# Threshold attention and a projection pair on one core: every other early slot's weights transposed by TensorE, copies to VectorE, loads and casts moved

## The chip, the core and the metric

The kernel runs on one core of a Trainium2 chip. A core has TensorE (PE: matrix products, results into PSUM), VectorE (DVE), ScalarE (ACT), GpSimd (POOL) and SyncE (SP), each with its own in-order queue, and 16 DMA engines that serve every queue. PSUM is divided into banks, which this kernel gives out by hand. The metric is the device time of one execution in microseconds (us); the median over several runs counts.

## What is computed

Eight batches of eight heads, 576 positions, head size 64. Attention keeps only the keys whose score is within tau of the row's maximum; the heads are put side by side and go through two projections with a hard swish between them.

```python
scores = scale * np.matmul(q, k.transpose(0, 1, 3, 2))
thresh = np.max(scores, axis=-1, keepdims=True) - tau
scores = np.where(scores >= thresh, scores, -1000000000.0)
scores = scores - np.max(scores, axis=-1, keepdims=True)
attn = np.exp(scores)
attn = attn / (np.sum(attn, axis=-1, keepdims=True) + 1e-09)
attn_out = np.matmul(attn, v)
# x: [8 * 576, 8 * 64], heads side by side
h = x @ w_in                      # [4608, 2048]
relu6 = np.clip(h + 3.0, 0.0, 6.0)
out = (h * relu6 / 6.0) @ w_out   # [4608, 512], float32
```

## The kernel before

Four heads of one batch form a *quad* (16 of them), two heads a *pair*. A quad has nine *slots*: slots 0 to 3 are the four tiles of 128 query rows of its first pair, 4 to 7 those of its second, and slot 8 holds the last 64 rows of both pairs. The main loop (L394) walks over all 144 slots, n from 0 to 143, and writes down by hand the order in which each engine gets its work; the tile framework only adds the semaphores. All engines run in order, so what is written earlier in the loop stands ahead on its engine.

In slot n the loop issues: the exponentials of slot n-1 (`sm_exp`, L262, ScalarE); the copy of slot n's scores out of PSUM with their row maximum (`sm_max`, L249, VectorE) and from it the bias of the mask (L252, GpSimd); if a batch is ready, one item of the first projection (`mm1` L315, `mm1_relu` L324/L326, `mm1_gate` L332); the reciprocal of slot n-1's sums (`sm_recip`, L265, VectorE); parts of the second projection (`mm2_part` L344, `mm2_out` L352); the mask of slot n (`sm_mask`, L257, ScalarE); one of the transposes of the next queries or keys, or a product of weights and values; the scores of slot n+1 (`scores`, L228/L234, TensorE); the scaling of slot n-1's weights to bf16 (`sm_norm`, L270, GpSimd) and their transpose.

That last transpose turns `pn`, 128 query rows by 2 x 576 keys in bf16, into nine blocks with keys on the partitions. It is one `dma_start_transpose` on SP's queue for each slot (L277), into `pts[pair]` or, for slot 8, `ptr[quad]`. Attention's second product reads these: `av_main(pair)` in slot 8 for a quad's first pair and in slot 3 of the next quad for its second pair, `av_rest(quad)` in slot 4 of the next quad (`av`, L285/L288).

Queries and keys of the first two batches are transposed by TensorE against an f32 identity (`main_pe` L185, `transpose_rest` L203/L205). `transpose_q` evicts with VectorE (L192), `transpose_k` and the keys of `transpose_rest` with ScalarE (L198, L210, L211). In slots 1, 2 and 5 to 7 of a quad this prepares the pairs to come.

PSUM: `ps_s` has two tiles of two banks for scores, `ps_h` one tile of two banks for the first projection, `ps_o` one bank for the second projection, `ps_m` one bank that transposes of queries and keys and the products with values share. The first projection has its first item in slot 23 (quad 2, slot 5), when the first batch is through; the second projection starts in slot 31. Until then `ps_h` and, but for one transpose ahead of the loop, `ps_o` stand unused.

Loads are queued as jobs and started at the end of a slot: `loads` on SP (two jobs a slot for n < 3, then one), `vcasts` (values, cast to bf16 on the way) and `casts` (16 pieces of w_in, then 16 of w_out) on GpSimd. GpSimd issues such a DMA in its own order, so the next slot's biases stand behind it. `load_quad(1)` queues its jobs in slot 0, `load_quad(quad + 2)` in slot 4 of each quad, `load_v(b + 1)` in slot 0 of each batch's second quad. Outputs wait in `late` and go out on SP in `flush`.

Of the kernel before, what the change touches and what calls it, by code (L numbers as in the profile page):

```python
# [9 lines left out]
F32 = mybir.dt.float32  # L10
BF16 = mybir.dt.bfloat16
# [4 lines left out]
P = 128  # L16
# [5 lines left out]
def kernel(  # L22
# [10 lines left out]
    nc = tc.nc  # L33
    B, H, S, D = q.shape
# [5 lines left out]
    NQUAD = B * H // 4  # L40
    NSLOT = 9
    NB = 2
    scale = 1.0 / math.sqrt(D)
    tau = float(tau)

    singles = ctx.enter_context(tc.tile_pool(name="singles", bufs=1))
# [4 lines left out]
    pn_pool = ctx.enter_context(tc.tile_pool(name="pn", bufs=4))  # L51
# [7 lines left out]
    ps_s = ctx.enter_context(tc.psum_pool(name="ps_s", bufs=2))  # L59
    ps_h = ctx.enter_context(tc.psum_pool(name="ps_h", bufs=1))  # L60
    ps_o = ctx.enter_context(tc.psum_pool(name="ps_o", bufs=1))
    ps_m = ctx.enter_context(tc.psum_pool(name="ps_m", bufs=1))
# [3 lines left out]
    nat = {}  # L66
    vsb = {}
    qkT = {}
    pts = {}
    ptr = {}  # L70
    xT = {}
    loads = []
    casts = []
    vcasts = []
# [3 lines left out]
    def load_quad(quad):  # L78
# [14 lines left out]
        def load_q(n):  # L93
            if b < NB:
                for a in range(2):
# [51 lines left out]
    def start(jobs, n):  # L147
        for _ in range(min(n, len(jobs))):
            jobs.pop(0)()
# [5 lines left out]

    identf = singles.tile([P, P], F32)
    make_identity(nc, identf)
    three = singles.tile([P, 1], F32)
    nc.vector.memset(three[:], 3.0)

# [6 lines left out]
    def alloc_qk(quad):  # L167
        qkT[quad] = (qk_pool.tile([P, 2, S], F32, tag="qT", name="qT"),
                     qk_pool.tile([P, 2, S + 64], F32, tag="kT", name="kT"))
# [4 lines left out]
    def kT_of(pair):  # L174
        return qkT[pair // 2][1][:, pair % 2, :]


    def by_pe(pair):
        return pair // NPAIR < NB

    def main_pe(src, pair, pool):
        ps = pool.tile([P, 512], F32, tag="m" if pool is ps_m else "o", name="tp")
        n = pair % 2
        for t in range(4):
            nc.tensor.transpose(ps[:, t * P:(t + 1) * P], src[:, t, 2 * n:2 * n + 2, :], identf[:])  # L185
        return ps

    def transpose_q(pair, pool=ps_m):
        nq = nat[pair // 2][0]
        if by_pe(pair):  # L190
            ps = main_pe(nq[:, 0:1024].rearrange("p (t h d) -> p t h d", h=4, t=4), pair, pool)
            return lambda: nc.vector.tensor_copy(out=qT_of(pair)[:, 0:512], in_=ps[:])  # L192
        n = pair % 2
        nc.vector.transpose(out=qT_of(pair), in_=nq[:, n * S:(n + 1) * S])

    def transpose_k(pair):
        ps = main_pe(nat[pair // 2][1], pair, ps_m)
        return lambda: nc.scalar.copy(out=kT_of(pair)[:, 64:576], in_=ps[:])  # L198

    def transpose_rest(quad):  # L200
        ps = ps_m.tile([P, 512], F32, tag="m", name="tr")
        nq, _, kr = nat[quad]
        nc.tensor.transpose(ps[:, 0:P], kr[:], identf[:])  # L203
        if by_pe(2 * quad):
            nc.tensor.transpose(ps[:, P:2 * P], nq[:, 1024:1152], identf[:])  # L205

        def evict():
            qT, kT = qkT[quad]
            both = ps[:].rearrange("p (w n t) -> p w n t", n=2, t=64)
            nc.scalar.copy(out=kT[0:64, :, S:S + 64], in_=both[0:64, 0])  # L210
            nc.scalar.copy(out=kT[64:P, :, 0:64], in_=both[64:P, 0])  # L211
            if by_pe(2 * quad):
                nc.vector.tensor_copy(out=qT[:, :, 512:S], in_=both[:, 1])  # L213
        return evict
# [49 lines left out]
    def sm_recip(sl):  # L264
        nc.vector.reciprocal(out=sl.rinv[:], in_=sl.rsum[:])  # L265

    def sm_norm(sl):
        pn = pn_pool.tile([P, 2, S], BF16, tag="pn", name="pn")
        for i in range(2):
            nc.gpsimd.tensor_scalar(out=pn[:, i, :], in0=sl.s[:, i, :], scalar1=sl.rinv[:, i:i + 1], scalar2=1.0,  # L270
                                    op0=Alu.mult, op1=Alu.mult)
        if sl.slot < 8:
            pair, t = 2 * sl.quad + sl.slot // 4, sl.slot % 4
            dst = pts[pair][:, :, t * P:(t + 1) * P]
        else:
            dst = ptr[sl.quad][:, :, :]
        nc.sync.dma_start_transpose(out=dst, in_=pn[:].rearrange("p a b -> p (a b)"))  # L277


    def av(ps, pair, pT, cols):  # L280
# [9 lines left out]
    def av_main(pair):  # L290
        b, hp = divmod(pair, NPAIR)
        if hp == 0:
            xT[b] = x_pool.tile([P, KI, S], BF16, tag="xT", name="xT")
        ps = ps_m.tile([P, 512], F32, tag="m", name="av")
        av(ps[:], pair, pts[pair], slice(0, 512))
        o0 = 64 if b % 2 else 0
        nc.vector.tensor_copy(out=xT[b][:, hp, o0:o0 + 512], in_=ps[:])  # L297

    def av_rest(quad):
        b, g = divmod(quad, 2)  # L300
        ps = ps_m.tile([P, 512], F32, tag="m", name="ar")
        for n in range(2):
            av(ps[:, n * 64:(n + 1) * 64], 2 * quad + n, ptr[quad], slice(n * 64, (n + 1) * 64))
        o0 = 0 if b % 2 else 512
        nc.vector.tensor_copy(out=xT[b][:, 2 * g:2 * g + 2, o0:o0 + 64],
                              in_=ps[:, 0:P].rearrange("p (a b) -> p a b", a=2))
# [69 lines left out]
        return items  # L376

    alloc_qk(0)
    evict = transpose_k(0)
    evict_q = transpose_q(0, ps_o)  # L380
    evict()
    evict_q()
    transpose_rest(0)()

    queue = []
    for quad in range(NQUAD):
        for slot in range(NSLOT):
            sl = Slot()
            sl.quad, sl.slot = quad, slot
            queue.append(sl)  # L390
    queue[0].tiles = scores(0, 0)

    prev = None
    for n, sl in enumerate(queue):  # L394
        quad, slot = sl.quad, sl.slot
        b, g = divmod(quad, 2)
        if slot in (0, 4):
            pts[2 * quad + slot // 4] = pt_pool.tile([P, 9, 512], BF16, tag="pT", name="pT")
        if slot == 8:
            ptr[quad] = ptr_pool.tile([P, 9, P], BF16, tag="pR", name="pR")  # L400
        if quad == 0 and slot == 0:
            load_quad(1)
        if slot == 4 and quad + 2 < NQUAD:
            load_quad(quad + 2)
        if slot == 0 and g == 1 and b + 1 < B:
            load_v(b + 1)
        if prev is not None:
            for i in range(2):
                sm_exp(prev, i)
        sm_max(sl)  # L410

        if slot != 8 and todo1:
            item, then = todo1.pop(0)
            h = mm1(item)
            r = mm1_relu(h, on_act=(slot in (0, 1, 3, 5)))
            mm1_gate(item, h, r)
            todo2.extend(then)
        if prev is not None:
            sm_recip(prev)
        outs = []  # L420
        for _ in range((2, 1, 1, 0, 1, 1, 1, 1, 1)[slot]):
            if todo2:
                bb, mt, part = todo2.pop(0)
                mm2_part(bb, mt, part)
                if part == 3:
                    outs += mm2_out(bb, mt, on_act=False)
        for i in range(2):
            sm_mask(sl, i)
        evict = None
        nxt = 2 * quad + 2  # L430
        if slot == 1:
            evict = transpose_q(2 * quad + 1)
        elif slot == 2:
            evict = transpose_k(2 * quad + 1)
        elif slot == 3 and quad > 0:
            av_main(2 * quad - 1)
        elif slot == 4 and quad > 0:
            av_rest(quad - 1)
            if quad % 2 == 0:
                todo1.extend(moe_of(quad // 2 - 1))  # L440
        elif slot in (5, 6, 7) and quad + 1 < NQUAD:
            if slot == 5:
                alloc_qk(quad + 1)
                evict = transpose_q(nxt)
            elif slot == 6:
                evict = transpose_k(nxt)
            else:
                evict = transpose_rest(quad + 1)
        elif slot == 8:
            av_main(2 * quad)  # L450
        if evict:
            evict()
        if n + 1 < len(queue):
            queue[n + 1].tiles = scores(queue[n + 1].quad, queue[n + 1].slot)
        if prev is not None:
            sm_norm(prev)
        flush()
        late.extend(outs)
        start(loads, 2 if n < 3 else 1)
        start(vcasts, 1 if n else 0)  # L460
        if n > 6:
            start(casts, 1 if n < 22 else 2)
        prev = sl

    for i in range(2):
# [6 lines left out]
    count = [0, 0]  # L472
# [59 lines left out]
```

## Time and profile before

| | us |
|---|---|
| median of 11 runs | 572.95 |
| lowest and highest | 571.73, 575.76 |
| the profiled execution, its time | 575.53 |
| the profiled execution, its span | 573.8 |
| PE busy in the span | 532.7 (93%) |
| ACT busy | 473.1 (82%) |
| DVE busy | 414.1 (72%) |
| POOL busy | 305.6 (53%) |

The span runs from the first to the last instruction of the program. Shares are averages over stages with different limits: the first slots, in which there is no projection yet, and those after the first batch. The slices of the page show it (each digit is a fortieth of the span, 14.3 us, in tenths; PEclk is the granted TensorE clock, DMA the share of the 16 DMA engines):

```profile
PE   6976788889999999998999999998999999999997
...
ACT  3987889688898999997898999988898999984440
...
PEclk9787889899999999999999999999999999999999
DMA  5999999998479787988489877988599775554101
```

The granted clock is below full in the first eight slices and the DMA engines are all but always busy there; from then on TensorE is at nine tenths.

| row of the page | count | busy, us | mean, ns |
|---|---|---|---|
| L228 PE, scores | 1024 | 181.0 | 451 |
| L249 DVE, scores out and maximum | 288 | 206.0 | 752 |
| L257 ACT, mask | 288 | 207.0 | 766 |
| L262 ACT, exponential | 288 | 192.9 | 672 |
| L270 POOL, scaling to bf16 | 288 | 211.6 | 745 |
| L185 PE, f32 transposes of keys | 128 | 20.9 | 289 |

The transposes by DMA are listed with the issues: 128 of pT, 3.5 us in the median from issue to landing.

### The profile page before, as it was taken

What the parts mean: (1) busy time and instruction counts of PE and PEld (TensorE: products, weight loads), DVE (VectorE), ACT (ScalarE), POOL (GpSimd) and SP (SyncE); (2) the same over time, 40 slices, a digit from 0 to 9 for tenths busy, and PEclk for the clock granted to TensorE, in tenths of its full rate; (3) what the DMA queues carried; (4) which work ended last, traced back from release to release, by engine and by line L of the source; (5) the groups of instructions that cost most, each with busy time, mean ns of one, the idle gap of its engine ahead of it and who ended that gap; (6) DMA issues with size and microseconds to landing.
All of it is one profiled execution on the core that took longest, in us unless ns stands there. A gap on an engine that the chain in (4) does not pass through costs nothing.

```text
span 573.8 us, 11332 instructions
## 1 busy us (share of the span) xinstructions
PE 532.7 (93%) x3700; PEld 303.9 (53%) x3700; DVE 414.1 (72%) x1020; ACT 473.1 (82%) x1008; POOL 305.6 (53%) x646
## 2 busy tenths in 40 slices
PE   6976788889999999998999999998999999999997
PEld 3543444554555555554555555554555555655663
DVE  2564557667887879886888888796878888884440
ACT  3987889688898999997898999988898999984440
POOL 0867778765556645654556655654556556552000
PEclk9787889899999999999999999999999999999999
DMA  5999999998479787988489877988599775554101
GB/s 119 142 163 169 186 180 164 183 187 168 98 141 183 130 141 154 165 156 159 90 162 156 156 140 156 187 134 146 108 172 152 152 150 97 128 88 111 39 19 74
DMA packets 298043, 80.45 MB, mean 140 GB/s; under 512 B 281088, under 2 KB 293376, under 8 KB 297984
## 3 DMA queue, kind: packets, MB, share of 16 engines
q1 hardware_dynamic: 280576, 70.81, 66.5%
q0 software_dynamic: 17408, 8.92, 12.8%
q8 instruction: 29, 0.48, 0.3%
q14 instruction: 30, 0.25, 0.1%
HBM read 36.70 MB, written 9.44 MB: 80 GB/s over the span
## 4 chain that ended last, share of the span: by engine, by line
PE 52%; ACT 12%; DVE 11%; issue 4%; DMA 3%; POOL 2%; SPq 1%; DVEq 0%; POOLq 0%
PE h L315 16%; PE o L344 15%; PE s L228 14%; DVE s L249 5%; ACT s L257 4%; ACT s L262 4%; PE av L285 3%; DVE g L332 2%; ACT r L324 2%; DVE r L326 2%; DMA pR<-pn 2%; DMA nq<-in_q_dram 2%; PE tp L185 1%; POOL pn L270 1%; DVE osb L352 1%
## 5 line engine op out<-in xcount | busy, mean ns | idle before, releaser
L270 POOL TENSOR_SCALAR pn<-s,rinv 128x576 bf16<-128x576 f32 x288 | 211.6, 745 | 135.3 <-DVE rinv L265 61.9
L249 DVE TENSOR_SCALAR_CACHE_REDUCE s<-s 128x576 f32<-128x576 f32 x288 | 206.0, 752 | 54.4 <-PE s L228 44.0
L257 ACT ACTIVATE s<-s,bias 128x576 f32<-128x576 f32 x288 | 207.0, 766 | 39.8 <-POOL bias L252 38.7
L262 ACT ACTIVATE s<-s 128x576 f32<-128x576 f32 x288 | 192.9, 672 | 0.4
L228 PE MATMUL s<-kT,qT 64*128 64x288 f32 x1024 | 181.0, 451 | 4.2 <-DVE s L249 3.4
L315 PE MATMUL h<-xT,w_in_sb 128*128 128x320 bf16 (+1 forms) x1024 | 145.8, 288 | 6.1 <-DVE g L332 5.2
L344 PE MATMUL o<-w_out_sb,g 128*128 128x512 bf16 x576 | 141.2, 379 | 6.5 <-DVE osb L352 5.9
L228 PEld LDWEIGHTS s<-kT,qT 64*128 64x128 f32 x1024 | 100.4, 196 | 64.6 <-DVE s L249 26.9
L315 PEld LDWEIGHTS <-w_in_sb 128*128 128x128 bf16 x1024 | 92.3, 98 | 69.8 <-issue 32.0
L332 DVE SCALAR_TENSOR_TENSOR g<-r,h 128x512 bf16<-128x512 f32 (+1 forms) x128 | 96.4, 755 | 41.4 <-ACT r L324 39.6
L252 POOL TENSOR_SCALAR bias<-m 128x1 f32<-128x1 f32 x288 | 54.7, 190 | 78.8 <-DVE s L249 57.4
L344 PEld LDWEIGHTS <-g 128*128 128x128 bf16 x576 | 55.5, 98 | 61.4 <-issue 13.2
L324 ACT ACTIVATE r<-h,three 128x640 f32<-128x640 f32 (+1 forms) x74 | 54.4, 736 | 27.1 <-PE h L315 26.5
L262 ACT ACTIVATION_READ_ACCUMULATOR s<-s 128x1 f32 x288 | 54.3, 189 | 0.0
L285 PE MATMUL av<-pT,vm 128*64 128x512 bf16 x256 | 36.0, 405 | 11.4 <-DVE qT L213 5.2
L326 DVE TENSOR_SCALAR r<-h 128x512 f32<-128x512 f32 (+1 forms) x54 | 40.5, 750 | 0.0
L285 PEld LDWEIGHTS <-vm 128*64 128x64 bf16 x512 | 18.9, 112 | 38.1 <-issue 26.6
L352 DVE TENSOR_SCALAR osb<-o 128x512 f32<-128x512 f32 x31 | 21.0, 676 | 22.2 <-PE o L344 22.2
L265 DVE RECIPROCAL rinv<-rsum 128x2 f32<-128x2 f32 x144 | 22.9, 159 | 12.2 <-ACT s L262 11.4
L297 DVE CAST xT<-av 128x512 bf16<-128x512 f32 x32 | 21.8, 682 | 9.3 <-PE av L288 9.2
L185 PE MATMUL tp<-identf,km 128*128 128x128 f32 x128 | 20.9, 289 | 4.8 <-DMA km<-in_k_dram 4.8
L249 DVE DVE_READ_ACCUMULATOR s<-s 128x1 f32 x288 | 23.9, 83 | 0.0
(34 smaller groups left out, 202.3 us busy)
## 6 DMA issues: line engine op xcount, KB each, us to landing
km<-in_k_dram SPq DMA_DIRECT2D x64, 128.0 KB, 3.0
out_dram<-osb SPq DMA_DIRECT2D x32, 256.0 KB, 2.4
nq<-in_q_dram SPq DMA_DIRECT2D x96, 72.0 KB, 2.7
vm<-in_v_dram POOLq DMA_DIRECT2D x16, 256.0 KB, 5.1
nq<-in_q_dram SPq DMA_DIRECT2D x16, 128.0 KB, 3.4
pT<-pn SPq DMA_TRANSPOSE x128, 3.5
w_in_sb<-in_moe_w_in_dram POOLq DMA_DIRECT2D x16, 128.0 KB, 4.5
w_out_sb<-in_moe_w_out_dram POOLq DMA_DIRECT2D x16, 128.0 KB, 5.1
```

The source lines that it names most:

```text
L228: nc.tensor.matmul(tiles[a][:, hf, 0:HALF], qT_of(pair)[a * 64:(a + 1) * 64, t * P:(t + 1) * P], keys(pair, a, hf), start=True, stop=True)
L249: nc.vector.tensor_scalar(out=sl.s[:, i, :].rearrange("p (a b) -> p a b", a=2), in0=ps[:, :, 0:HALF], scalar1=1.0, scalar2=None, op0=Alu.m ...
L252: nc.gpsimd.tensor_scalar(out=sl.bias[:, i:i + 1], in0=sl.m[:, i:i + 1], scalar1=-scale, scalar2=tau, op0=Alu.mult, op1=Alu.add)
L257: nc.scalar.activation(out=s, in_=s, func=Act.Prelu, bias=sl.bias[:, i:i + 1], scale=scale, alpha=REJECT)
L262: nc.scalar.activation(out=s, in_=s, func=Act.Exp, accum_out=sl.rsum[:, i:i + 1])
L270: nc.gpsimd.tensor_scalar(out=pn[:, i, :], in0=sl.s[:, i, :], scalar1=sl.rinv[:, i:i + 1], scalar2=1.0, op0=Alu.mult, op1=Alu.mult)
L285: nc.tensor.matmul(ps[a * 64:(a + 1) * 64, :], vm[:, 2 * hp + a, c * D:(c + 1) * D], pT[:, 5 * a + c, cols], start=(c == 0), stop=False)
L315: nc.tensor.matmul(hps[:, n, 0:w], w_in_sb[:, ki, (ni + n) * P:(ni + n + 1) * P], xT[b][:, ki, c0:c0 + w], start=(ki == 0), stop=(ki == KI ...
L324: nc.scalar.activation(out=r, in_=hps, func=Act.Relu, bias=three[:])
L326: nc.vector.tensor_scalar(out=r, in0=hps, scalar1=3.0, scalar2=0.0, op0=Alu.add, op1=Alu.max)
L332: nc.vector.scalar_tensor_tensor(out=gbuf[:, ni:ni + 2, c0:c0 + w], in0=r, scalar=6.0, in1=hps, op0=Alu.min, op1=Alu.mult)
L344: nc.tensor.matmul(o_ps[0], gbuf[:, ni, mt * P:(mt + 1) * P], w_out_sb[:, ni, :], start=(ni == 0), stop=(ni == NI - 1))
```

## The change

The weights of every odd slot among the first 22 (n = 1, 3, ... 21) are no longer transposed by DMA. `pe_transpose`, called two slots later between the projection's item and the reciprocal, has TensorE transpose the nine blocks of `pn` against a bf16 identity into the two banks of `ps_h`, and VectorE copies all 1152 columns out in one instruction behind the reciprocal. The other slots keep their DMA transpose.

`bank` replaces the fixed `ps_m`: while n < 28 the transposes of queries and keys and the products with values take `ps_o` and `ps_m` in turn. `copy_out` moves the evictions of the keys from ScalarE to VectorE for 0 <= n < 22.

Ahead of the loop TensorE gets 14 f32 transposes of the identity with a result that nothing reads, and four more between the first keys and the first queries. GpSimd copies one column of the first transposed keys into `gate`, and behind it starts all four loads of the first batch's values. In the loop values are then started only for n > 12; pieces of w_in and w_out are started from n = 0, two a slot for n < 4 and one from there (before: none up to n = 6, one up to n = 21, then two). `load_quad(2)` is called in slot 8 of quad 0 instead of slot 4.

```diff
--- before.py
+++ after.py
@@ -40,6 +40,8 @@
     NQUAD = B * H // 4
     NSLOT = 9
     NB = 2
+    N1 = 22
+    N2 = 28
     scale = 1.0 / math.sqrt(D)
     tau = float(tau)
 
@@ -155,6 +157,16 @@
 
     identf = singles.tile([P, P], F32)
     make_identity(nc, identf)
+
+    warm = ps_s.tile([P, 2, 512], F32, tag="s", name="warm")
+
+    def warm_up(count):
+        for _ in range(count):
+            nc.tensor.transpose(warm[:, 0, 0:P], identf[:], identf[:])
+
+    warm_up(14)
+    identb = singles.tile([P, P], BF16)
+    nc.vector.tensor_copy(out=identb[:], in_=identf[:])
     three = singles.tile([P, 1], F32)
     nc.vector.memset(three[:], 3.0)
 
@@ -174,31 +186,48 @@
     def kT_of(pair):
         return qkT[pair // 2][1][:, pair % 2, :]
 
+    now = -1
+    turn = 0
+
+    def bank(name):
+        nonlocal turn
+        turn += 1
+        if now < N2 and turn % 2:
+            return ps_o.tile([P, 512], F32, tag="o", name=name)
+        return ps_m.tile([P, 512], F32, tag="m", name=name)
+
+
+    def copy_out(out, in_):
+        if 0 <= now < N1:
+            nc.vector.tensor_copy(out=out, in_=in_)
+        else:
+            nc.scalar.copy(out=out, in_=in_)
+
 
     def by_pe(pair):
         return pair // NPAIR < NB
 
-    def main_pe(src, pair, pool):
-        ps = pool.tile([P, 512], F32, tag="m" if pool is ps_m else "o", name="tp")
+    def main_pe(src, pair):
+        ps = bank("tp")
         n = pair % 2
         for t in range(4):
             nc.tensor.transpose(ps[:, t * P:(t + 1) * P], src[:, t, 2 * n:2 * n + 2, :], identf[:])
         return ps
 
-    def transpose_q(pair, pool=ps_m):
+    def transpose_q(pair):
         nq = nat[pair // 2][0]
         if by_pe(pair):
-            ps = main_pe(nq[:, 0:1024].rearrange("p (t h d) -> p t h d", h=4, t=4), pair, pool)
+            ps = main_pe(nq[:, 0:1024].rearrange("p (t h d) -> p t h d", h=4, t=4), pair)
             return lambda: nc.vector.tensor_copy(out=qT_of(pair)[:, 0:512], in_=ps[:])
         n = pair % 2
         nc.vector.transpose(out=qT_of(pair), in_=nq[:, n * S:(n + 1) * S])
 
     def transpose_k(pair):
-        ps = main_pe(nat[pair // 2][1], pair, ps_m)
-        return lambda: nc.scalar.copy(out=kT_of(pair)[:, 64:576], in_=ps[:])
+        ps = main_pe(nat[pair // 2][1], pair)
+        return lambda: copy_out(kT_of(pair)[:, 64:576], ps[:])
 
     def transpose_rest(quad):
-        ps = ps_m.tile([P, 512], F32, tag="m", name="tr")
+        ps = bank("tr")
         nq, _, kr = nat[quad]
         nc.tensor.transpose(ps[:, 0:P], kr[:], identf[:])
         if by_pe(2 * quad):
@@ -207,8 +236,8 @@
         def evict():
             qT, kT = qkT[quad]
             both = ps[:].rearrange("p (w n t) -> p w n t", n=2, t=64)
-            nc.scalar.copy(out=kT[0:64, :, S:S + 64], in_=both[0:64, 0])
-            nc.scalar.copy(out=kT[64:P, :, 0:64], in_=both[64:P, 0])
+            copy_out(kT[0:64, :, S:S + 64], both[0:64, 0])
+            copy_out(kT[64:P, :, 0:64], both[64:P, 0])
             if by_pe(2 * quad):
                 nc.vector.tensor_copy(out=qT[:, :, 512:S], in_=both[:, 1])
         return evict
@@ -265,16 +294,26 @@
         nc.vector.reciprocal(out=sl.rinv[:], in_=sl.rsum[:])
 
     def sm_norm(sl):
-        pn = pn_pool.tile([P, 2, S], BF16, tag="pn", name="pn")
+        sl.pn = pn = pn_pool.tile([P, 2, S], BF16, tag="pn", name="pn")
         for i in range(2):
             nc.gpsimd.tensor_scalar(out=pn[:, i, :], in0=sl.s[:, i, :], scalar1=sl.rinv[:, i:i + 1], scalar2=1.0,
                                     op0=Alu.mult, op1=Alu.mult)
         if sl.slot < 8:
             pair, t = 2 * sl.quad + sl.slot // 4, sl.slot % 4
-            dst = pts[pair][:, :, t * P:(t + 1) * P]
+            sl.dst = pts[pair][:, :, t * P:(t + 1) * P]
         else:
-            dst = ptr[sl.quad][:, :, :]
-        nc.sync.dma_start_transpose(out=dst, in_=pn[:].rearrange("p a b -> p (a b)"))
+            sl.dst = ptr[sl.quad][:, :, :]
+        if not sl.on_chip:
+            nc.sync.dma_start_transpose(out=sl.dst, in_=pn[:].rearrange("p a b -> p (a b)"))
+
+
+    def pe_transpose(sl):
+        ps = ps_h.tile([P, 2, 1024], BF16, tag="h", name="pt")
+        ps = ps[:].rearrange("p a b -> p (a b)")[:, 0:2 * S].rearrange("p (c t) -> p c t", t=P)
+        pn = sl.pn[:].rearrange("p a b -> p (a b)")
+        for c in range(9):
+            nc.tensor.transpose(ps[:, c, :], pn[:, c * P:(c + 1) * P], identb[:])
+        return lambda: nc.vector.tensor_copy(out=sl.dst, in_=ps)
 
 
     def av(ps, pair, pT, cols):
@@ -291,14 +330,14 @@
         b, hp = divmod(pair, NPAIR)
         if hp == 0:
             xT[b] = x_pool.tile([P, KI, S], BF16, tag="xT", name="xT")
-        ps = ps_m.tile([P, 512], F32, tag="m", name="av")
+        ps = bank("av")
         av(ps[:], pair, pts[pair], slice(0, 512))
         o0 = 64 if b % 2 else 0
         nc.vector.tensor_copy(out=xT[b][:, hp, o0:o0 + 512], in_=ps[:])
 
     def av_rest(quad):
         b, g = divmod(quad, 2)
-        ps = ps_m.tile([P, 512], F32, tag="m", name="ar")
+        ps = bank("ar")
         for n in range(2):
             av(ps[:, n * 64:(n + 1) * 64], 2 * quad + n, ptr[quad], slice(n * 64, (n + 1) * 64))
         o0 = 0 if b % 2 else 512
@@ -376,17 +415,23 @@
         return items
 
     alloc_qk(0)
+    gate = singles.tile([P, 1], F32)
     evict = transpose_k(0)
-    evict_q = transpose_q(0, ps_o)
+    warm_up(4)
+    evict_q = transpose_q(0)
     evict()
     evict_q()
     transpose_rest(0)()
+
+    nc.gpsimd.tensor_copy(out=gate[:], in_=kT_of(0)[:, 64:65])
+    start(vcasts, 4)
 
     queue = []
     for quad in range(NQUAD):
         for slot in range(NSLOT):
             sl = Slot()
             sl.quad, sl.slot = quad, slot
+            sl.on_chip = len(queue) < N1 and len(queue) % 2 == 1
             queue.append(sl)
     queue[0].tiles = scores(0, 0)
 
@@ -394,13 +439,14 @@
     for n, sl in enumerate(queue):
         quad, slot = sl.quad, sl.slot
         b, g = divmod(quad, 2)
+        now = n
         if slot in (0, 4):
             pts[2 * quad + slot // 4] = pt_pool.tile([P, 9, 512], BF16, tag="pT", name="pT")
         if slot == 8:
             ptr[quad] = ptr_pool.tile([P, 9, P], BF16, tag="pR", name="pR")
         if quad == 0 and slot == 0:
             load_quad(1)
-        if slot == 4 and quad + 2 < NQUAD:
+        if slot == (4 if quad else 8) and quad + 2 < NQUAD:
             load_quad(quad + 2)
         if slot == 0 and g == 1 and b + 1 < B:
             load_v(b + 1)
@@ -415,8 +461,11 @@
             r = mm1_relu(h, on_act=(slot in (0, 1, 3, 5)))
             mm1_gate(item, h, r)
             todo2.extend(then)
+        copies = pe_transpose(queue[n - 2]) if n > 1 and queue[n - 2].on_chip else None
         if prev is not None:
             sm_recip(prev)
+        if copies:
+            copies()
         outs = []
         for _ in range((2, 1, 1, 0, 1, 1, 1, 1, 1)[slot]):
             if todo2:
@@ -457,9 +506,8 @@
         flush()
         late.extend(outs)
         start(loads, 2 if n < 3 else 1)
-        start(vcasts, 1 if n else 0)
-        if n > 6:
-            start(casts, 1 if n < 22 else 2)
+        start(vcasts, 1 if n > 12 else 0)
+        start(casts, 2 if n < 4 else 1)
         prev = sl
 
     for i in range(2):
```

## The prediction

> **What bounds the kernel now.** I read the stages first: a single-number share of the span mixes two regimes. Columns: length, busy us of PE, PE's weight loads, VectorE (DVE), ScalarE (ACT) and GpSimd (POOL) with instruction counts, granted TensorE clock, DMA share, GB/s.
>
> ```profile
> 10.00:38.00 28.00, 24.52 (x112) 13.62 (x109) 16.14 (x48) 25.24 (x55) 18.20 (x39) 0.88 0.92 153
> 38.00:71.00 33.00, 24.74 (x138) 13.96 (x138) 17.13 (x51) 25.97 (x59) 23.74 (x50) 0.79 1.20 170
> 71.00:84.00 13.00, 10.53 (x51) 5.71 (x50) 7.54 (x22) 12.76 (x29) 10.70 (x22) 0.88 1.06 169
> 84.00:103.00 19.00, 15.77 (x117) 9.06 (x114) 12.42 (x34) 15.32 (x34) 14.53 (x30) 0.86 1.29 176
> 137.00:514.00 377.00, 368.63 (x2715) 209.94 (x2713) 311.99 (x762) 340.58 (x735) 209.89 (x446) 1.00 0.78 143
> ```
>
> From 137 to 514 us TensorE is busy 368.63 of 377 us at full clock: it is the bound, and the change doesn't touch it (3.49 us a slot, 108 slots). By VectorE's maxima (L249) slots 0 to 21 run from 10.4 to 84.6 us, 74.2 us, 3.37 a slot: here no engine is full, the clock is granted at 0.79 to 0.88, and the DMA share exceeds 1. The projections start at slot 23, so the time of slots 0 to 21 lies wholly before the bound stage and comes off the end one for one.
>
> Next, who waits in 10 to 85 us (total, times, longest):
>
> ```profile
> DVE s L249 <- PE s L228: 13.3, 13, 1.9
> ACT s L257 <- POOL bias L252: 11.1, 11, 2.8
> PE av L285 <- DMA pT<-pn: 4.1, 2, 2.4
> PE av L285 <- DVE qT L213: 3.2, 2, 1.8
> PEld L285 <- DMA pR<-pn: 2.5, 1, 2.5
> ```
>
> ScalarE is the busiest (63.97 of the 74 us from 10 to 84), its idle time ends on bias, bias on VectorE's maximum, that on the scores. What makes the scores late shows in the timeline (start, length, engine, instruction):
>
> ```profile
> 45.14 4.96 SPq L277 DMA_TRANSPOSE pR<-pn  x1
> ...
> 50.20 9.21 SPq L277 DMA_TRANSPOSE pT<-pn  x4
> ...
> 50.29 1.92 PE L285 MATMUL av<-pT,vm 128*64 128x512 bf16 x8 [2.42 <-DMA pT<-pn]
> ...
> 55.44 1.45 ACT L257 ACTIVATE s<-s,bias 128x576 f32<-128x576 f32 x2 [2.80 <-POOL bias L252]
> ```
>
> TensorE's queue is in order: attention's second product waits for a transposed tile that the DMA rings deliver late (5.3 us median to landing up to 137 us, 11.2 at worst, against 3.4 afterwards), and the next scores stand behind it. Slots 12, 13 and 21 stretch to 6.7, 4.7 and 6.2 us that way.
>
> **The change, part by part.** Sums are against the profiled execution: span 573.8 us, 575.53 with what lies around it, 2.6 above the median of 572.95; a difference carries over to the median.
>
> *Half the transposes leave DMA.* Eleven of the first 22 (odd slots). Each is 128x1152 bf16, 1152 rows of 256 B; at the DMA queues' mean of 23 ns a packet that is 26 us of packet time, 1.65 us of all 16 engines, so 18 us of a ring that is over-full here. It also takes eleven blocking SP issues away, ahead of which loads and the other transposes queue. I expect the landings to fall to about 4 us and the waits at slots 12, 13 and 21 to go. On ScalarE these were 2.8, 1.9 and 1.7 us: **-4.7 in slots 0 to 21, -1.7 in slot 22.** What is late next: ScalarE itself.
>
> *TensorE gets 11 x 9 bf16 transposes.* No row shows one. Nearest are four f32 ones (L185): 0.44 us on the chain of waits at full clock, 1.11 at half; and a 128-column bf16 weight load, 98 ns (L344). Nine cost 0.9 us at full clock, 1.9 at half. The Trainium skill, "TensorE: Matmul & The Clock Gate", Part 4, speaks against this: about 275 ns for one 128x128 bf16 transpose in a kernel. By that 11 x 9 x 0.275 = 27 us, more than all that there is to win; but L185's mean of 289 ns is such a duration too, and four take 0.44 us from first to last, because they are pipelined. I take 0.9 (bounds 0.9 and 2.5), 10 us over 11 slots. Does it fit? TensorE's work per quad at full clock: nine slots of scores at 1.24 (timeline, from 88.7 us) = 11.2; four f32 transposes at 0.6 and two small ones, 2.9; two main products at 1.45 and a rest one, 3.5; 4.5 transposed slots, 4.0. That is 21.6, 2.4 a slot: inside ScalarE's cycle, if the clock is full.
>
> *VectorE copies them out, 11 x 1152 bf16 from PSUM,* and takes over key copies. From PSUM, 128x512 f32 took 0.69 us and 128x128 0.29 (L192, L213): 1.04 ns an element and 0.16 fixed, so 1.36 us for 1152. "VectorE: DVE Perf Modes", "Why PSUM operands drop a tier", allows two a cycle with 16-bit elements from PSUM: 0.76. No row here shows a 16-bit PSUM source; I take 0.76, because both ends of the copy are bf16 with unit runs, and keep 1.36. VectorE per quad: maxima 9 x 1.45, reciprocals 1.45, query copies 1.65, key copies 1.86, products out 1.67, new copies 4.5 x 0.76 = 3.4: 23.1, or 2.6 a slot; at 1.36 it is 2.9, just over ScalarE's 2.73. Queued behind the copy, which waits for TensorE, are the query and key evictions and the next maximum. The loop exponential, reciprocal, GpSimd's scaling (1.5), transposes (0.9), scores, maximum, bias, mask sums to about 9 us for three slots, 3.0 a slot in the slots concerned. I book **+2.0** for such waits over 22 slots (bounds 0 and 6).
>
> *ScalarE's key copies go* for slots 0 to 21: five of 0.58 and four of 0.25 us, 3.9 us of the engine with the least slack (63.97 - 3.9 = 60.1, 2.73 a slot): **-3.9**.
>
> *Alternating banks* in slots 0 to 27. Today the product of slot 8 waits in ps_m for the small evictions that stand behind ScalarE's masks: "PE av L285 <- DVE qT L213" in slots 8, 17 and 26, 5.2 us in all. The first two are partly counted above; slot 26 gives **-1.5**.
>
> *Casts smoothed.* A w_in issue takes GpSimd 0.57 us. Four first v issues (0.83, 0.83, 0.65, 0.65) move ahead of slot 0, behind the gate on kT, near 7 us; they end near 10, ahead of the first bias at 11.24: hidden with 1 us to spare, and 1 us late at most if that cover goes. Slots 0 to 3 then carry two casts, 1.15 instead of 0.65 to 0.93: with two biases (0.38) and scaling (1.47) 3.0 us a slot against 2.3 to 3.3 now, **+0.8**. In slots 22 to 30 one cast instead of two saves GpSimd 0.57 a slot, where bias makes ScalarE wait 7.2 us (84 to 137 us) and products and projections share the cold stretch from 97.9 to 104.7 us: **-2.5**. The third quad's loads start four slots later, at slot 8, and are due at slot 14: hidden.
>
> *Warm-up.* Fourteen f32 transposes before the data, four between keys and queries. At 0.278 us each they run from about 1.4 to 5.3 us, and the keys landed at 4.77: half a us late, then 1.1 us for the four, +1.5 if the clock stays low. If they raise it, the first scores take 1.5 instead of 2.97 us and slots 0 and 1 gain: -3. The same page says that transpose mode doesn't count as busy for the clock. Around the clock's changes this trace has:
>
> ```profile
> 19.40:22.80 3.40, 2.30 (x11) 1.26 (x10) 2.53 (x8) 3.38 (x9) 2.92 (x6) 1.00 1.35 170
> 22.80:26.20 3.40, 3.40 (x12) 1.89 (x10) 1.89 (x7) 3.40 (x9) 3.15 (x7) 0.50 1.39 237
> 26.20:29.60 3.40, 3.40 (x14) 1.93 (x13) 1.64 (x5) 3.30 (x8) 2.12 (x6) 0.50 1.20 215
> ...
> 56.90:60.30 3.40, 3.40 (x13) 2.04 (x14) 1.50 (x4) 1.47 (x5) 1.75 (x4) 0.50 1.14 229
> ```
>
> A stretch with TensorE busy 2.30 of 3.40 us is followed by half clock; 56.9 to 60.3 us, full, with a us of transposes in it, by full clock. So transposes don't prevent a rise; whether they help none of these rows tells. I take **-0.5** for the start (bounds -3 and +1.5).
>
> **Sum:** -4.7 -1.7 +2.0 -3.9 -1.5 +0.8 -2.5 -0.5 = -12.0, less 1 for slots where two of these name the same wait: -11. The span becomes 562.8 and the median 572.95 - 11 = **562**.
>
> **Rivals.**
> 1. *VectorE or GpSimd becomes the bound of the stage.* With 1.36 us copies VectorE needs 2.9 a slot before any wait, and its order ties it to TensorE and GpSimd; at 3.2 a slot, 70.4 us, only 3.8 of the 74.2 go, and with 1 from later slots it is 568. For: all four engines lie between 2.4 and 2.7. Against: VectorE idles nearly half the stage now.
> 2. *Slower: TensorE is cold and becomes the bound.* If bf16 transposes don't count for the clock gate, counted work at ScalarE's pace is (21.6 - 4.0)/9/2.73 = 72% full, at the edge of the 2.30/3.40 = 68% after which the clock halved. Cold work costs double: with a share f of the 2.4 us done cold a slot needs 2.4(1 + f), past today's 3.37 at f = 0.40. At f = 0.55 it is 3.72, 81.8 us, +7.6, of which casts and banks return 2: 578.5. For: the clock of 0.79 in 38 to 71 us. Against: three of the drops followed DMA waits that go.
> 3. *The transposes were hidden anyway.* Other work fills in and new waits replace the old: 572.5. For: the rings are also fed by loads and casts. Against: three waits end on pT or pR by name.
>
> **Chances.** Forecast 0.58, rival 1 0.17, rival 2 0.20, rival 3 0.05. About 0.2%, 1.1 us, can be told from no change. Faster: 0.58 + 0.17 less a little at rival 1's edge = 0.74; slower: 0.20 and half of rival 3, 0.22; same 0.04. Forecast's own range is 556 to 568 (unknown costs -6 to +6); the range reaches to 574 to take in rival 1 and half of rival 3, and leaves the cold case out.
>
> **What would show it.** Right: slots 0 to 21 take 62 to 66 us, pT lands within 4 us there, no wait of L285 on pT or pR at slots 12, 13 and 21, nine transposes in 0.9 us, copies of 0.76. The clock from 38 to 71 us rises above 0.79. Wrong: copies at 1.36; a clock below 0.8 with TensorE near full (rival 2); ScalarE's waits on bias staying near 11 us with other names behind them; the scores of slot 0 later than 8.06 us.

## The result and the profile after

The changed kernel takes 568.81 us in the median of 12 runs (565.78 to 570.9), the kernel before 573.08 us (570.17 to 580.03). The ratio is 0.992 with a 95% interval of 0.9902 to 0.9939: faster by 4.6 us (3.5 to 5.6) by the ratio, 4.3 us by the medians, where 11 were forecast.

The two profiled executions differ by more: spans of 573.8 and 566.2 us, 7.5 us apart. The kernel before was profiled in an execution of 575.53 us, 2.4 above its median, the changed one in one of 568.0, 0.8 below its own. The profile says where time went; how much is said by the ratios.

The slices of the page after, to be laid beside those of before:

```profile
PE   7898788999999999998999999998999999999997
...
PEclk9899998999999999999999999999999999999999
DMA  7999969977689867976589879987789975553101
```

The clock is better in the first eight slices (before: 97878898), TensorE is fuller; from the ninth slice on the clock is full in both pages. The stages, with the columns of the prediction's table:

```profile
10.00:38.00 28.00, 23.21 (x138) 13.56 (x139) 19.68 (x56) 23.70 (x51) 21.10 (x46) 0.88 1.15 160
38.00:71.00 33.00, 27.45 (x210) 15.99 (x210) 26.04 (x72) 30.27 (x67) 29.25 (x61) 0.96 1.22 185
71.00:84.00 13.00, 10.24 (x84) 5.67 (x81) 9.03 (x25) 10.89 (x25) 7.98 (x19) 0.96 0.65 110
```

From 38 to 71 us ScalarE is now busy 30.27 of 33 us (25.97 before) and the clock is granted at 0.96 (0.79 before). From 10 to 38 us nothing is better: ScalarE does less than before, and the DMA share has risen from 0.92 to 1.15.

Slot by slot, from the start of the first row maximum of each slot in the timeline (L249 before, L278 after):

| slots | before, us | after, us | slots that changed most (before, after) |
|---|---|---|---|
| up to slot 0 | 10.38 | 9.55 | |
| 0 to 8 | 27.75 | 28.03 | 0 (3.14, 2.30), 1 (3.28, 4.92) |
| 9 to 17 | 32.97 | 27.51 | 12 (6.69, 2.38), 13 (4.71, 3.13), 17 (2.69, 4.38) |
| 18 to 21 | 13.49 | 13.43 | 19 (2.51, 4.77), 21 (6.23, 3.90) |
| 22 to 35 | 52.72 | 50.61 | 23 (3.36, 5.36), 26 (4.83, 2.48), 30 (6.13, 4.78) |
| 36 to 142 | 377.14 | 377.14 | |
| from the last maximum to the end | 59.30 | 59.96 | |

The three DMA waits are gone and their 8.2 us with them. But other slots grew: 1, 17, 19 and 23. In slot 1 TensorE waits for queries from DMA, in slot 17 for GpSimd's pn (1.4 us), in slot 23 for a tile of PSUM; the experiments below take these up. Slot 19 lies in a stretch at half clock, 68.6 to 72.0 us. Every kept profile has such stretches in its first 120 us, of 3.4 us or a multiple of it and in varying places; one of 3.4 us takes 0.003 off the mean clock over 566 us. And the stage from slot 36 on takes the same time to 0.01 us: what is won ahead of it comes off the end one for one.

Who waits now in slots 0 to 21 (total, times, longest):

```profile
PEld L315 <- POOL pn L299: 11.5, 20, 1.6
...
ACT s L286 <- POOL bias L281: 10.0, 14, 2.1
...
PE pt L315 <- POOL pn L299: 5.7, 14, 1.1
```

No product (L324) waits for a pT or pR any more. ScalarE still stands 10.0 us (11.1 before). Behind it seems to lie another cause: TensorE itself, in front of the transposes (L315), waits for GpSimd's pn.

### The profile page after: what moved, and what is told of

Its sections match the earlier page's. It is cut to its first block, busy times and chain, and to the rows that moved or that the text cites. A ratio compares the mean times of both kernels' runs of the same rounds, so it can differ in the third digit from the quotient of the medians.

```text
span 566.2 us, 11556 instructions
## 1 busy us (share of the span) xinstructions
PE 532.9 (94%) x3817; PEld 307.4 (54%) x3817; DVE 425.5 (75%) x1041; ACT 469.7 (83%) x999; POOL 305.7 (54%) x647
## 4 chain that ended last, share of the span: by engine, by line
PE 54%; DVE 14%; ACT 9%; issue 3%; DMA 3%; SPq 2%; POOL 0%; DVEq 0%
PE o L383 16%; PE h L354 16%; PE s L257 15%; DVE s L278 6%; ACT s L286 4%; PE av L324 3%; ACT s L291 3%; DVE g L371 3%; DVE r L365 2%; DMA nq<-in_q_dram 2%; ACT r L363 2%; PE tp L214 1%; DVE osb L391 1%; PE s L263 1%; SPq L307 1%
## 5 line engine op out<-in xcount | busy, mean ns | idle before, releaser
L278 DVE TENSOR_SCALAR_CACHE_REDUCE s<-s 128x576 f32<-128x576 f32 x288 | 205.9, 752 | 44.8 <-PE s L257 35.7
L257 PE MATMUL s<-kT,qT 64*128 64x288 f32 x1024 | 173.6, 438 | 6.0 <-DVE s L278 5.5
L257 PEld LDWEIGHTS s<-kT,qT 64*128 64x128 f32 x1024 | 96.0, 189 | 62.6 <-DVE s L278 26.9
L324 PE MATMUL av<-pT,vm 128*64 128x512 bf16 x256 | 33.7, 385 | 0.5 <-ACT kT L204 0.4
L324 PEld LDWEIGHTS <-vm 128*64 128x64 bf16 x512 | 17.9, 110 | 23.6 <-issue 16.6
L278 DVE DVE_READ_ACCUMULATOR s<-s 128x1 f32 x288 | 23.9, 83 | 0.0
L389 ACT ACTIVATE osb<-o 128x512 f32<-128x512 f32 x5 | 3.0, 597 | 23.9 <-PE o L383 23.9
```

What stands on the lines that cost most here:

```text
L257: nc.tensor.matmul(tiles[a][:, hf, 0:HALF], qT_of(pair)[a * 64:(a + 1) * 64, t * P:(t + 1) * P], keys(pair, a, hf), start=True, stop=True)
L278: nc.vector.tensor_scalar(out=sl.s[:, i, :].rearrange("p (a b) -> p a b", a=2), in0=ps[:, :, 0:HALF], scalar1=1.0, scalar2=None, op0=Alu.m ...
L324: nc.tensor.matmul(ps[a * 64:(a + 1) * 64, :], vm[:, 2 * hp + a, c * D:(c + 1) * D], pT[:, 5 * a + c, cols], start=(c == 0), stop=False)
```

## The experiments

All kernels were timed in five rounds beside the kernel before on the same chip. The ratio is to that kernel; medians of different groups of runs lie on different chips, whose medians of before range from 573.6 to 574.6 us.

### TensorE transposes alone, and everything else without them

The changed kernel with every transpose by DMA:

```diff
-            sl.on_chip = len(queue) < N1 and len(queue) % 2 == 1
+            sl.on_chip = False
```

> The changed kernel with all weights transposed by DMA again, everything else kept. Theory A (the gain of the change comes from the three DMA waits of slots 12, 13 and 21): these waits are back and the median is near 573, as before the change. Theory B (the other parts, key copies, banks, casts, carry the gain): it stays at 568 to 569, or below if the TensorE transposes cost more than they bring.

Measured: 573.08 us, ratio 0.9985 (0.996 to 1.0011). The other five parts (banks, key copies, warm-up, values and casts, `load_quad(2)`) are worth nothing on balance without the transposes. The profile is of a long execution, 577.59 us: slots 22 to 35 take 47.8 us (52.7 before), but slots 17 and 21 take 12.6 and 7.7, with TensorE waiting 11.0 us for a pT, and the clock is at half from 58.0 to 81.9 us.

The kernel before with `identb`, `pe_transpose` and its copy, and nothing else of the change:

```diff
-        nc.sync.dma_start_transpose(out=dst, in_=pn[:].rearrange("p a b -> p (a b)"))
+        if not sl.on_chip:
+            nc.sync.dma_start_transpose(out=sl.dst, in_=pn[:].rearrange("p a b -> p (a b)"))
...
+        copies = pe_transpose(queue[n - 2]) if n > 1 and queue[n - 2].on_chip else None
         if prev is not None:
             sm_recip(prev)
+        if copies:
+            copies()
```

> The kernel before with nothing but the TensorE transposes of the odd slots. Theory A: they alone bring most of the 4.3 us, 569 to 570. Theory B: they are worth nothing by themselves, 573, or cost time where ps_m, key copies on ScalarE and casts are as before.

Measured: 571.15 us, ratio 0.9941 (0.9918 to 0.9964). By themselves they bring 3.4 of the 4.6 us (2.7 by the medians). So most of the gain needs the transposes; the question was why it is small.

They also go with a better clock. The mean granted clock of an execution is 0.976 in the median of the kernel before (75 executions beside these experiments), 0.964 to 0.982 in the changed kernel without the transposes, 0.990 to 1.000 in the kernel with nothing else, 0.988 in the median of the changed kernel. Of executions with the same clock, 0.981 to 0.983, eleven of the kernel before have a median of 572.2 us and four of the changed kernel one of 570.4: 1.9 us. So more than half of the 4.6 us goes along with fewer stretches at half clock. Whether those were a consequence of the waits on DMA, as three of them in the profile before followed such waits, no run separates.

### The wait for pn

```diff
-        copies = pe_transpose(queue[n - 2]) if n > 1 and queue[n - 2].on_chip else None
+        copies = pe_transpose(queue[n - 3]) if n > 2 and queue[n - 3].on_chip else None
```

> The changed kernel with each TensorE transpose issued three slots after its slot instead of two. Theory A (TensorE stands waiting for GpSimd's pn, and the next scores behind it, which eats what the DMA waits gave back): the waits of L315 on POOL pn (17 us in 10 to 79 us) all but go, slots 0 to 21 fall from 69.0 to 64-66 us and the median from 568.8 to 565 or less. Theory B (the stage is set by ScalarE and by the work of four nearly full engines): the waits move elsewhere, stage and median stay within 1 us.

Measured: 566.38 us, ratio 0.9866 (0.9836 to 0.9895), 2.4 us faster than the changed kernel by the medians, 3.1 by the ratios. Slots 0 to 21 take 65.3 us instead of 69.0. The same transposes (of slot 13) in the changed kernel's timeline, TensorE alone:

```profile
54.80 0.40 PE L315 MATMUL pt<-identb,pn 128*128 128x128 bf16 x4 [0.38 <-POOL pn L299]
55.52 0.45 PE L315 MATMUL pt<-identb,pn 128*128 128x128 bf16 x5 [0.33 <-POOL pn L299]
```

and one slot later, in this one:

```profile
55.91 0.68 PE L315 MATMUL pt<-identb,pn 128*128 128x128 bf16 x9
```

In the first, TensorE waits for the first half of pn, transposes four blocks, waits for the second half; the next scores stand behind both. In the second the nine run through. L315's waits on pn fall from 17.2 us to 1.6 (slots 0 to 21), ScalarE's on bias from 10.0 to 7.6. Theory A holds for the waits and the stage; the median stayed above the 565 that it named. Slot 21's transposes now stand in slot 24, which takes 6.35 us instead of 2.76.

### Slot 21 and the first projection

Slot 23 of the changed kernel, TensorE's rows and the one VectorE row that they wait for:

```profile
81.18 1.05 PE L354 MATMUL h<-xT,w_in_sb 128*128 128x256 bf16 x8
83.13 0.69 DVE L371 SCALAR_TENSOR_TENSOR g<-r,h 128x512 bf16<-128x512 f32 x1 [0.78 <-ACT r L363]
83.87 0.66 PE L315 MATMUL pt<-identb,pn 128*128 128x128 bf16 x9 [1.64 <-DVE g L371]
84.37 0.61 PE L214 MATMUL tp<-identf,nq 128*128 128x128 f32 x4
```

Slot 23 has the first item of the projection, `mm1`, and the loop writes it ahead of `pe_transpose`. Both want the only tile of `ps_h`. So slot 21's transposes wait until ScalarE and VectorE have emptied the projection's result, and the next queries and scores wait behind them.

```diff
-            sl.on_chip = len(queue) < N1 and len(queue) % 2 == 1
+            sl.on_chip = len(queue) < 20 and len(queue) % 2 == 1
```

> The changed kernel with TensorE transposes for odd slots up to 19 only; slot 21 goes by DMA. Theory C (slot 21's transposes share ps_h with the first projection, which is written ahead of them in slot 23, and TensorE waits 1.64 us there for the hard swish): slot 23 falls from 5.36 to about 3.4 us, the median by 1 to 2 us to 567-568. Rival: the DMA transpose of slot 21 makes a later product wait instead, 568.8.

Measured: 565.23 us, ratio 0.9837 (0.9813 to 0.986): 3.6 us faster than the changed kernel by the medians, 4.8 by the ratios, for one slot's transposes fewer, and more than the 1 to 2 us expected. The slot as it is now:

```profile
81.61 1.05 PE L354 MATMUL h<-xT,w_in_sb 128*128 128x256 bf16 x8
82.50 0.60 PE L214 MATMUL tp<-identf,nq 128*128 128x128 f32 x4
83.03 1.24 PE L257 MATMUL s<-kT,qT 64*128 64x288 f32 x8
```

Slot 23 falls from 5.36 to 3.50 us, as expected. That is 1.9 us, and all that the traces put on this wait. The rest goes at least in part with the clock. The changed kernel's profile is at half clock in slots 19 and 27 (68.6 to 72.0, 95.9 to 99.3 us), this one in slot 17 (62.2 to 65.6). So slots 19 and 27 are shorter here by 1.6 and 1.3 us, but slot 17 is longer by 1.2 and slot 1 by 0.8. Slots 1, 17 and 19 end before slot 21's transposes would begin, so that these differences can't be the edit's doing. Of executions with the same mean clock, 0.991, three of the changed kernel took 566.85 to 568.26 us and three of this one 565.18 to 565.28; eight of the changed kernel's twelve lie at 0.989 or lower, none of these five. Whether slot 23 brings about the stretch near 96 us isn't settled: the kernels of e13, e14 and e16 below, also without slot 21, had one between 92.6 and 100.0 us.

> Both of the above: transposes three slots later, up to slot 19. If the waits on pn (theory A) and the wait in ps_h (theory C) are two separate losses, they add up: 566.4 - 2 = 564.5, with slot 24 back from 6.35 to 2.8 us. If they are one slack counted twice: 566 to 567.

Both edits together: 563.84 us, ratio 0.9812 (0.9788 to 0.9836), the lowest median here. This is below the 564.5 that stood for two separate losses. But slot 21 had turned out to be worth 3.6, and by the medians the delay is worth 2.4 us with slot 21 and 1.4 without it, the latter not clear of noise (the ratios' intervals overlap): if they add up, then only in part.

> The kernel before with nothing but the TensorE transposes, of odd slots up to 19. If slot 21 alone spoilt the change (theory C), the transposes by themselves bring most of what the changed kernel up to slot 19 brings (9.3 us): 566 to 568. If the other parts (banks, key copies, casts) carry weight once slot 21 is out of the way, 569 to 570.5.

The kernel before with the transposes alone, up to slot 19: 569.77 us, ratio 0.9933 (0.991 to 0.9957), by the ratio no better than with slot 21 (0.9941; 571.15 us). So the rival held: theory C's sum fell. Slot 23 did shrink, from 5.22 to 3.36 us, and slots 22 to 35 together from 53.5 to 52.2, but slot 26 grew from 3.39 to 4.34 and slots 30 and 31 by 1.6 us, with stretches at half clock now over them (92.5 to 95.9, 109.5 to 112.9 us). So the other parts, which could be taken from the changed kernel one by one at no loss (below), carry some 4.5 us by the medians, 5.5 by the ratios, once slot 21 is out.

### Key copies and banks

Key evictions on ScalarE (`copy_out`), and ps_m alone (`bank`), each first with slot 21 as it is and then without it:

```diff
-        if 0 <= now < N1:
+        if False:
```

```diff
-    N2 = 28
+    N2 = 0
```

> The changed kernel with the key evictions left on ScalarE. My prediction gave their move -3.9 us, so the median would rise to 572.7. Rival (ScalarE waits 10 us in slots 0 to 21 anyway, and what it does in that time is hidden): within 1 us of 568.8.

> The changed kernel with ps_m alone from slot 0 on (the alternation kept only ahead of the loop). My prediction gave the banks -1.5 in slot 26 and part of slots 8 and 17: the median would rise to 570.5-572. Rival (the chain through ps_m was ended by key copies on ScalarE, and with these on VectorE one bank is enough): 569, but slot 26 longer by 2 us.

Measured: 567.66 us, 0.9909 (0.9879 to 0.9938), and 567.88 us, 0.9905 (0.9876 to 0.9934). Neither is slower than the changed kernel's 568.81; in that both rivals held. The 2 us expected in slot 26 with ps_m alone didn't come: 2.70 against 2.48.

> TensorE transposes up to slot 19 and the key evictions back on ScalarE. If ScalarE sets the stage once slot 21 is out of the way (my -3.9): 568 to 569. If its waits hide them as they did with slot 21 in: 565 to 566.

> TensorE transposes up to slot 19 and ps_m alone. If the chain through the one bank is what slot 26 lost in the kernel with nothing but the transposes (4.34 against 2.47 us): 567. If it was ScalarE's key copies or the pairs of casts: 565 to 566, slot 26 at 2.5 to 2.7.

> TensorE transposes up to slot 19, ps_m alone and key evictions on ScalarE: both at once. If one covers for the other (the single bank only hurts where its emptying stands behind ScalarE's masks), this is slower than either by itself: 567 to 568, slots 8, 17 and 26 longer by 1 to 2 us. If neither matters: 565 to 566.

Against 565.23 us: key copies on ScalarE 567.35 (0.9892, 0.9852 to 0.9932), ps_m alone 566.79 (0.9893, 0.9849 to 0.9937), both 568.18 (0.9902, 0.9867 to 0.9937). The first two intervals overlap that of 0.9837, but of the executions none does: the five of the comparison run from 564.94 to 565.96 us, those of the three kernels start at 566.15, 566.59 and 566.5. By the medians the copies carry about 2.1 us, the banks 1.6, both together 3.0; by the ratios 3.2, 3.2 and 3.7. With ps_m alone slot 26 takes 4.32 instead of 2.47 us, the place that the prediction named:

```profile
92.55 1.92 PE L324 MATMUL av<-pT,vm 128*64 128x512 bf16 x8 [1.98 <-DVE qT L242]
```

The wait is there, but only half of the story: the products behind it run at half clock (92.6 to 96.0 us). With slot 21 in place (e6) the same wait, 2.1 us there, was followed by full clock, and slot 26 took 2.70.

### Loads and casts, and the warm-up

```diff
-    nc.gpsimd.tensor_copy(out=gate[:], in_=kT_of(0)[:, 64:65])
-    start(vcasts, 4)
...
-        if slot == (4 if quad else 8) and quad + 2 < NQUAD:
+        if slot == 4 and quad + 2 < NQUAD:
...
-        start(vcasts, 1 if n > 12 else 0)
-        start(casts, 2 if n < 4 else 1)
+        start(vcasts, 1 if n else 0)
+        if n > 6:
+            start(casts, 1 if n < 22 else 2)
```

> The changed kernel with values, casts and the third quad's loads started as before the change, without the gate. My prediction gave the smoothing +0.8 in slots 0 to 3 and -2.5 in slots 22 to 30: the median would rise by 1.7 to 570.5. Rival: the early casts only crowd the rings while the first quad's second half is loading (TensorE waited 1.4 us for nq in slot 1), and later casts were hidden: 567 to 568.5, with slot 1 shorter by 1.5 us.

Measured: 567.2 us, 0.9889 (0.986 to 0.9919), not slower than the changed kernel; the rival held. Slot 1 is 2.30 us instead of 4.92. The reason shows in the issues of 5 to 15 us (KB each, median us to landing), first of the changed kernel:

```profile
vm<-in_v_dram POOLq DMA_DIRECT2D x2, 256.0 KB, 6.2
nq<-in_q_dram SPq DMA_DIRECT2D x4, 128.0 KB, 6.2
w_in_sb<-in_moe_w_in_dram POOLq DMA_DIRECT2D x2, 128.0 KB, 6.4
```

then with the old order:

```profile
nq<-in_q_dram SPq DMA_DIRECT2D x4, 128.0 KB, 2.9
```

The queries of the first quad's second pair share the rings with six early transfers of GpSimd (two more, vr, are not shown) and land in 6.2 instead of 2.9 us; TensorE waits for them in slot 1 (1.4 us) and everything behind it, and from 14.0 to 17.4 us it then runs at half clock.

> TensorE transposes up to slot 19 with loads and casts as before. If the pairs of casts cost the late slots their 4.6 us (22 to 36: 52.2 against 47.5): slots 22 to 36 at 50 to 52, less 3 in slot 1, so 565 to 567. If the late slots stay at 47.5 to 48, it is faster than with early casts: 562 to 563.

Without slot 21: 565.01 us, 0.9849 (0.9809 to 0.9889), beside 565.23. A zero, made of two parts: slots 0 to 8 take 24.6 instead of 29.0 us, slots 22 to 35 51.3 instead of 47.5. Stretches at half clock are in both differences (the profile with the new order has them from 14.4 and 28.1 us on, that with the old from 90.6 and 104.2).

The 18 transposes of the identity ahead of the loop left out (both calls of `warm_up` and the tile), with the new order of loads and with the old:

> The changed kernel without its 18 transposes ahead of the loop. My prediction gave them -0.5: 569.3. If they bring the clock up early, as the first scores (1.56 us instead of 2.97) suggest, the first maximum comes at 10.4 instead of 9.55 us and slot 1 is longer: 570.5 to 571.5. If slot 1 waits for nq from DMA in any case, what they win is lost there: 568.8.

> The changed kernel with loads and casts as before and without the transposes ahead of the loop. If the warm-up wins 3 us that the early casts take back in slot 1, this one is 3 us slower than the same kernel with warm-up: 570 (first maximum at 10.4 us, slots 0 and 1 at 3.1 and 3.3). If the warm-up brings nothing, 567.

Measured: with the new order 569.08 us, 0.9923 (0.9893 to 0.9953), no difference from 568.81. With the old order 570.52, 0.9923 (0.9902 to 0.9945), 3.3 us slower than with the warm-up (567.2), 2.0 by the ratios; in the profiles slots 0 and 1 and what lies ahead of them are 2.6 us longer. So the warm-up wins 2 to 3 us with the old order. Why it wins nothing with the new one is open. Slot 1's wait for nq doesn't take it back: it is 1.4 us with and without the warm-up, and without it slot 2 still begins 2.1 us later. In these two profiles 1.6 of that comes back in slot 19, which is at half clock in the changed kernel alone.

### Attempts at the best of all

> Transposes three slots later and up to slot 19, values from slot 1 on, casts from slot 3 on (two a slot up to slot 5, then one), no gate. If slot 1's wait for nq is the early casts' doing and the late pairs of casts cost slots 30 and 32 their 2 us, this gets both: 561 to 563. Rival (slot 1's 2.5 us return as a wait of a later slot): 564.5.

> Everything that paid by itself: transposes three slots later and up to slot 19, warm-up, key copies, banks; values from slot 1 on, no cast before slot 5, one a slot then, two in slots 16 to 21, one up to slot 30. If slot 1's wait (3 us or more) can be avoided without paying for it in slots 5 to 8 or 30: 561 to 562.5. If the stage is at its floor by ScalarE and GpSimd: 563.5 to 564.

The two had the delay, the limit at slot 19, values from slot 1 on, no gate, and the casts placed as said: `start(casts, 0 if n < 3 else 2 if n < 6 else 1)` and `start(casts, 0 if n < 5 else 2 if 15 < n < 22 else 1)`. Measured: 564.14 us (0.9816, 0.9794 to 0.9837) and 564.5 us (0.9817, 0.9793 to 0.9841). Neither is faster than the 563.84 above; the rivals were right in that. Slot 1 is 2.30 us in both, but in the first slots 6 to 8 are 4.5, 3.7 and 3.6, and in the second slots 22 to 35 take 51.8 us instead of the 48.1 of e9. What the first slots give comes back later. That ScalarE and GpSimd set a floor there, the rival's reason in e17, wasn't tested.

## Why the prediction was right in sign and wrong in size

**The step that failed** is "TensorE gets 11 x 9 bf16 transposes" with its "Does it fit?". It held TensorE's work per quad against ScalarE's time and found room. It didn't ask for the tile that the result goes into. Ten of the eleven slots find `ps_h` empty; the eleventh, slot 21, is transposed in slot 23, behind the first projection in program order, and waits there for the hard swish: 1.64 us, and slot 23 is 1.9 us longer for it. Without this one slot's transposes the change is worth 9.3 us (ratio 0.9837; 8.0 to 10.7), within the forecast's own range. Of the 4.8 us between the two ratios the wait itself is 1.9; the rest goes at least in part with the clock, and why isn't settled.

**A second step failed**, "a difference carries over to the median". From profile to profile the span did fall by 7.5 us, but by the ratios the change is worth 4.6. The profiled execution of before was 2.4 us above its median, and since the full stage takes the same time in every profile, the excess can hardly lie but in the stage that was to shrink. Nor had the sum a term of its own for stretches at half clock within the loop.

**DMA waits, -4.7 and -1.7: right in kind.** The waits of slots 12, 13 and 21 are gone, and the transposes alone bring 3.4 us. One reading was wrong: the landings didn't fall to 4 us. Up to 79 us their median is still 5.2, and 8.8 at worst (11.2 before). So the waits ended without a median that fell. What may have ended them: a slot that TensorE transposes no longer depends on the rings (slot 7, ahead of slot 12, is one), and the transposes that stay are issued earlier, slot 8's at 41.1 instead of 45.1 us.

**Waits of the loop, +2.0: right.** The loop through GpSimd's scaling was named; a slot's delay gives 2.4 us back, 1.4 without slot 21. VectorE's copies took 0.74 us, the lower of the two prices (0.76), and nine transposes 0.87 us of TensorE (8.7 us for 90), 0.9 in the sum. By the 275 ns apiece of the Trainium skill ("TensorE: Matmul & The Clock Gate", Part 4) nine would have taken 2.5.

**Key copies, -3.9, and banks, -1.5: behind another wait.** With slot 21 in place neither showed a gain. Without it each is worth 1.6 to 3.2 us (medians and ratios), 3.0 to 3.7 together, where 5.4 were booked. The copies were booked as if ScalarE never waited; that this is why the sum was too large is likely but not shown.

**Casts, +0.8 and -2.5: the late part right, the early part mis-sized.** Slots 25 and 28 to 32, at full clock in the changed kernel's profile and in that with the old order, differ by 2.9 us. The early part was far too small: 2.2 us in slots 0 to 8 (28.0 against 25.8), 4.4 without slot 21. I had counted GpSimd's issue time and called it hidden; the cost was in the rings, where nq for slot 1 was in flight, a transfer that the sum left out.

**Warm-up, -0.5:** 3.3 us by the medians with the old order of loads, near the bound of -3, and nothing with the new order. The sum for the start left the loads out, too; whether they are the reason is open.

**Rivals.** The cold TensorE didn't come about: the clock in 38 to 71 us rose from 0.79 to 0.96. The edge of 68% busy that it was judged by didn't hold: half clock followed a stretch with 2.40 of 3.40 us busy (65.2 to 68.6 us of the changed kernel), full clock one with 1.95 (89.5 to 92.9 us without slot 21). VectorE's copy was at the fast price, so rival 1's mechanism didn't decide, though its time, 568, is near the measured one. The transposes by DMA were not hidden (e3).

## What to carry to other kernels

Before work is moved into a resource that "stands idle", list by program order who takes that resource next: leaving out one late user of eleven was worth 3.6 us here beside a gain of 4.6, and with it in place the other parts showed no worth. A part that can be taken out at no loss may only stand behind a larger wait; take it out again once that wait is gone. A transfer that is started earlier isn't free because its issue is hidden: ask which load it shares the rings with, and when that load is due. And where executions differ in their clock, compare those with the same clock before a wait is made to pay for a whole difference.

## What the runs showed of the hardware

The clock went up on transposes alone. Here is TensorE ahead of the first scores in the changed kernel, which has issued nothing but f32 transposes until then:

```profile
5.80 1.06 PE L165 MATMUL warm<-identf 128*128 128x128 f32 x4
6.66 0.84 PE L214 MATMUL tp<-identf,nq 128*128 128x128 f32 x4
7.33 0.27 PE L232 MATMUL tr<-identf,kr 128*128 128x128 f32 x1
```

Single transposes (L232) take 0.27 us where they took 0.42 before the change (L203), and the eight score products behind them 1.56 us instead of 2.97. In the changed kernel without the warm-up they take 0.42 and 2.97 again. So these f32 transposes do raise the clock. The Trainium skill's "TensorE: Matmul & The Clock Gate" (Part 4) says otherwise of transpose mode; the trace calls the rows MATMUL and doesn't tell the mode. And in 38 to 71 us, with six slots' bf16 transposes in it, the clock was at 0.96.

A stage at its limit repeats closely: slots 36 to 142 took 377.1 to 377.2 us in the profiles of all kernels, with the clock at full. All that tells the kernels' profiles apart lies in the first 130 us and, by 0.7 us, in the tail.
